# Column sums of a Sinkhorn loop taken by VectorE ahead of a product of ones, and a closing branch's transfers put on GpSimd's queue

## The chip, the cores and the metric

The kernel runs on one core of a Trainium2 chip. The metric is the device time of one execution in microseconds (us). Before the change it is 1538.89 us, the median of three runs (1538.41 to 1539.11).

A core has five engines that each run their own list of instructions in program order and wait for one another by semaphores: TensorE (PE in the profile, with its weight loads as PEld), VectorE (DVE), ScalarE (ACT), GpSimd (POOL) and SyncE (SP), which here only starts transfers. Transfers (DMAs) are started from the list of an engine; SP's and GpSimd's lists are the two that matter here.

## The reference, cut to what matters

A recurrence over 768 steps (linear attention with 4 batches, 8 heads of 48) gives `x`, 3072 tokens of 384. A mixture of 8 experts follows, whose gate matrix `P` (3072 x 8) is balanced by eight rounds of Sinkhorn:

```python
logits = x @ w_gate
logits = logits - logits.max()
P = np.exp(logits)
for _ in range(8):
    P /= P.sum(1, keepdims=True) + 1e-09
    P /= P.sum(0, keepdims=True) + 1e-09
    P *= N / E
out = np.zeros((N, D), dtype=np.float32)
for e in range(E):
    h = np.maximum(x @ w1[e], 0.0)
    ye = h @ w2[e]
    out += P[:, e:e + 1] * ye
```

The first division in a round is by sums over the 8 experts of a token (row sums), the second by sums over all 3072 tokens for each expert (column sums).

## The kernel before, in words

The kernel has four stretches. The **attention** runs over 24 chunks of 128 tokens, and beside it the first expert begins. The **ticks** follow: a list of units of TensorE work of the first expert is emptied one unit a tick, and small jobs are attached to tick numbers. The 14 **stages** come next: each is half of one of the other seven experts, done with 15 products of combined operands for the first matrix (a Strassen-like scheme, `g1_slots`, 30 slots for each of two groups of tokens) and plain products for the second (`g2_tiles`). Last stands the **closing branch**, `general`, a plain and slow version of everything, which is entered only when `flag` says that a decay `w` lies outside 0.7 to 1.1. The inputs draw `w` from 0.85 to 0.95.

Every engine is wrapped so that its instructions stay in the order in which the code is written (`InOrder`). So the code's order is the engine's order, and an instruction that waits holds up everything behind it on its engine.

`pm` holds the gate matrix as 128 partitions x (24 tiles x 8 experts). The generator `sinkhorn_rounds` makes a round in two pieces that are divided by `yield`. The first piece, all VectorE: row sums `rs`, their reciprocals, and `pm` times these. The second piece: the column sums `cs`, their reciprocals, and `pm` times these. Column sums cross partitions, which is done by a TensorE product with a matrix of ones (`pc`); the sums over the 24 tiles are VectorE's.

The pieces are not run in one go. In the ticks, `next(sk)` is called at ticks 0, 1, 2, 3, 4, 7, 9, 12, 14, 17, 19, 22, 24, 27, 29 and 32 (line 917); the first four set up the exponentials, so rounds 0 to 5 have their first pieces at 4, 9, 14, 19, 24, 29 and their second at 7, 12, 17, 22, 27, 32. Rounds 6 and 7 lie in stage 0, at slots 2, 5, 9 and 13 (line 1131), and slot 18 ends the loop. Three ticks of TensorE work, or three to four slots, lie between the end of a first piece and the second one.

The units of the ticks alternate. A unit `ph` (`g1_unit`) is nine products of 384 columns; its end is read by ScalarE (a Relu into `hb`) and then by VectorE (`SCALAR_TENSOR_TENSOR hb<-ph,hb`, the rest that the Relu's 16-bit result leaves). A unit `po` (`g2_half`) is twelve products, read by ScalarE alone. So a unit's VectorE instruction is issued behind its products and stands in VectorE's list ahead of whatever the next tick gives to VectorE. In stage 0 the products are named `bA`, `bY`, `bZ`, `bC`, `bB`, and VectorE's additions on them `tb`. VectorE has other work in the ticks too: low parts of split operands (`xv`, later `ws`) and maxima of the weights (`wms`).

The times below call the eight second pieces round 0 to round 7.

Of the kernel before, what the change touches and what calls it, by code (L numbers as in the profile page):

```python
# [8 lines left out]
F32 = mybir.dt.float32  # L9
# [4 lines left out]
ALU = mybir.AluOpType  # L14
AX = mybir.AxisListType
# [18 lines left out]
def rwkv_sinkhorn_moe(  # L34
# [13 lines left out]
    V, S_, G, T, Q = (  # L48
        InOrder(tc, e) for e in (nc.vector, nc.scalar, nc.gpsimd, nc.tensor, nc.sync)
    )  # L50

    B, H, S, D = r.shape
    NT, DM = out.shape
    E, _, F = w1.shape
    P = 128
# [3 lines left out]
    NTT = NT // P  # L59
    KC = DM // P  # L60
    FC = F // P
    TB = 512
# [25 lines left out]
    def part(home, dtype, at, shape):  # L88

        n = 1  # L90
        for s_ in shape:
            n *= s_
        x_ = home if home.dtype == dtype else home.bitcast(dtype)
        x_ = x_[:, at : at + n]
        if len(shape) == 1:
            return x_
        names = "abcd"[: len(shape)]
        return x_.rearrange(
            f"p ({' '.join(names)}) -> p {' '.join(names)}", **{c_: s_ for c_, s_ in zip(names[1:], shape[1:])}
        )  # L100
# [17 lines left out]
    logits = const.tile([P, NTT, E], F32, name="logits")  # L118
# [4 lines left out]
    ones = const.tile([P, P], F32, name="ones")  # L123
# [255 lines left out]
    for src, dst in ((tab, rtab), (tabr, ktab)):  # L379
        pt = ps3.tile([P, NPAIR, P], F32, tag="pa", name="pt_tab")  # L380
# [7 lines left out]
        out=mask, in_=mask, compare_op=ALU.is_gt, fill=0.0, base=0,  # L388
# [376 lines left out]
    pm = const.tile([P, NTT, E], F32, name="pm")  # L765
# [83 lines left out]
    skp = [ps4, "pq"]  # L849
# [27 lines left out]
    def sinkhorn_rounds(nm):  # L877
        for it in range(8):
            rs = sm.tile([P, NTT], F32, tag="rs", name=f"rs_{nm}{it}")
            V.tensor_reduce(rs, pm, axis=AX.X, op=ALU.add)  # L880
            V.tensor_scalar_add(rs, rs, 1e-9)
            V.reciprocal(rs, rs)
            V.tensor_tensor(pm, pm, rs.unsqueeze(2).broadcast_to([P, NTT, E]), op=ALU.mult)
            yield
            pc = skp[0].tile([P, NTT, E], F32, tag=skp[1], name=f"pc_{nm}{it}")
            T.matmul(
                pc.rearrange("p t e -> p (t e)"), ones, pm.rearrange("p t e -> p (t e)"),
                start=True, stop=True,
            )
            cs = sm.tile([P, E], F32, tag="cs", name=f"cs_{nm}{it}")  # L890
            V.tensor_reduce(cs, pc.rearrange("p t e -> p e t"), axis=AX.X, op=ALU.add)
            V.tensor_scalar(cs, cs, 1e-9, E / NT, op0=ALU.add, op1=ALU.mult)
            V.reciprocal(cs, cs)
            V.tensor_tensor(pm, pm, cs.unsqueeze(1).broadcast_to([P, NTT, E]), op=ALU.mult)
            yield
# [297 lines left out]
    def general(scratch):  # L1193

        BH = B * H
        yd = scratch.tile([B, S, DM], F32, name="yd")
        ldr = scratch.tile([NT, E], F32, name="ldr")
        pdr = scratch.tile([NT, E], F32, name="pdr")
        kb, rb, stt, kv = (part(hbx, F32, i * BH * D, (BH, D))[:D] for i in range(4))
        wn, un = (part(hbx, F32, 4 * BH * D + i * H * D, (H * D,))[:D] for i in range(2))  # L1200
        vt, yv = (part(hbx, F32, 5 * BH * D + i * BH, (BH,))[:D] for i in range(2))
        for dst, src in ((wn, w), (un, u)):
            Q.dma_start(dst, src.rearrange("(o h) d -> o (h d)", o=1).broadcast_to([D, H * D]))
        V.memset(stt, 0.0)

        def of_b(x_):
            return x_.rearrange("p (b h) d -> p b (h d)", b=B)

        def for_b(x_):
            return x_.unsqueeze(1).broadcast_to([D, B, H * D])  # L1210

        with tc.For_i(0, S, 1) as t:
            for dst, src in ((kb, k), (rb, r)):
                Q.dma_start(
                    dst,
                    src.rearrange("b h s d -> s (b h) d")[bass.ds(t, 1)].broadcast_to([D, BH, D]),
                )
            Q.dma_start(vt, v.rearrange("b h s d -> s d (b h)")[bass.ds(t, 1)].rearrange("o d a -> (o d) a"))
            V.tensor_tensor(kv, kb, vt.unsqueeze(2).broadcast_to([D, BH, D]), op=ALU.mult)
            V.tensor_tensor(of_b(kb), of_b(kv), for_b(un), op=ALU.mult)  # L1220
            V.tensor_tensor(kb, kb, stt, op=ALU.add)
            V.tensor_tensor(rb, rb, kb, op=ALU.mult)
            V.tensor_reduce(yv, rb, axis=AX.X, op=ALU.add)
            for b in range(B):
                Q.dma_start(
                    yd[b].rearrange("s (h d) -> s d h", d=D)[bass.ds(t, 1)].rearrange("o d h -> (o d) h"),
                    yv[:, b * H : (b + 1) * H],
                )
            V.tensor_tensor(of_b(stt), of_b(stt), for_b(wn), op=ALU.mult)
            V.tensor_tensor(stt, stt, kv, op=ALU.add)  # L1230

        def tiles_of(x_):
            return x_.rearrange("(t p) d -> t p d", p=P)

        yt = tiles_of(yd.rearrange("b s d -> (b s) d"))
        xt = part(hb3, F32, 0, (DM,))
        xT = part(hb3, F32, DM, (KC, P))
        acc = part(hb3, F32, 2 * DM, (DM,))
        wgf = part(hb3, F32, 3 * DM, (KC, E))
        lt, pt = (part(hb3, F32, 3 * DM + (KC + i) * E, (E,)) for i in range(2))  # L1240
        raw_a, raw_b = part(ws0, F32, 0, (KC, F)), part(ws1, F32, 0, (FC, DM))
        hT = part(hbx, F32, 0, (FC, P))
        Q.dma_start(wgf, w_gate.rearrange("(c p) e -> p c e", p=P))

        def turned(t):
            Q.dma_start(xt, yt[bass.ds(t, 1)].rearrange("o p d -> (o p) d"))
            px = ps1.tile([P, KC, P], F32, tag="ph", name="px_g")
            for c in range(KC):
                T.transpose(px[:, c], xt[:, c * P : (c + 1) * P], ident)
            S_.copy(xT, px)  # L1250

        with tc.For_i(0, NTT, 1) as t:
            turned(t)
            pl = ps2.tile([P, E], F32, tag="po", name="pl_g")
            for c in range(KC):
                T.matmul(pl, xT[:, c], wgf[:, c], start=(c == 0), stop=(c == KC - 1))
            S_.copy(lt, pl)
            Q.dma_start(tiles_of(ldr)[bass.ds(t, 1)].rearrange("o p d -> (o p) d"), lt)
        Q.dma_start(logits, ldr.rearrange("(t p) e -> p t e", p=P))
        mx = sm.tile([P, 1], F32, tag="mx", name="mx_g")  # L1260
        gm = sm.tile([P, 1], F32, tag="gm", name="gm_g")
        V.tensor_reduce(mx, logits, axis=AX.XY, op=ALU.max)
        for all_ in over_partitions(mx, 1, ps1, "ph", "gm_g"):
            pass
        V.tensor_scalar(gm, all_, -1.0, 0.0, op0=ALU.mult, op1=ALU.add)
        S_.activation(pm, logits, AF.Exp, bias=gm, scale=1.0)
        for _ in sinkhorn_rounds("g"):
            pass
        Q.dma_start(pdr.rearrange("(t p) e -> p t e", p=P), pm)
        with tc.For_i(0, NTT, 1) as t:  # L1270
            turned(t)
            Q.dma_start(pt, tiles_of(pdr)[bass.ds(t, 1)].rearrange("o p d -> (o p) d"))
            V.memset(acc, 0.0)
            for e in range(E):
                Q.dma_start(raw_a, w1[e].rearrange("(c p) f -> p c f", p=P))
                Q.dma_start(raw_b, w2[e].rearrange("(c p) d -> p c d", p=P))
                for f in range(FC):
                    ph = ps1.tile([P, P], F32, tag="ph", name=f"ph_g{e}_{f}")
                    for c in range(KC):
                        T.matmul(  # L1280
                            ph, raw_a[:, c, f * P : (f + 1) * P], xT[:, c],
                            start=(c == 0), stop=(c == KC - 1),
                        )
                    S_.activation(hT[:, f], ph, AF.Relu)
                po = ps2.tile([P, DM], F32, tag="po", name=f"po_g{e}")
                for f in range(FC):
                    T.matmul(po, hT[:, f], raw_b[:, f], start=(f == 0), stop=(f == FC - 1))
                V.scalar_tensor_tensor(acc, po, pt[:, e : e + 1], acc, op0=ALU.mult, op1=ALU.add)
            Q.dma_start(tiles_of(out)[bass.ds(t, 1)].rearrange("o p d -> (o p) d"), acc)

    bad = nc.values_load(flag.bitcast(I32), min_val=0, max_val=0x3F800000)
    with tc.If(bad > 0, preferred_fallthrough_block=False):
# [29 lines left out]
```

## Time and profile before

| | |
|---|---|
| median of three runs | 1538.89 us |
| the profiled execution, its own time | 1539.2 us |
| its span in the trace | 1537.5 us |
| TensorE busy | 1520.4 us (99% of the span) |
| VectorE busy | 1007.9 us (66%) |
| ScalarE busy | 678.4 us (44%) |
| GpSimd busy | 567.3 us (37%) |
| mean granted TensorE clock | 0.993 |

The span is the time from the first to the last instruction of the program; the 1.7 us that the execution's own time has beyond it lie around the program. The 40 slices show how even the kernel is, and that TensorE's clock is below full only in the first two:

```profile
PE   8999999999999999999999999999999999999998
DVE  7887667676666666667666666666666666566563
PEclk8899999999999999999999999999999999999999
```

Each digit is the busy share of a slice of 38 us in tenths; the last row is the clock granted to TensorE. A matmul's row in a timeline is modelled: its start is the time at which it enters the array, and the next one enters before it ends, so the spacing of starts is what a product costs TensorE.

### The profile page before, as it was taken

How to read it: one execution, taken by the hardware profiler on the slowest of the kernel's cores; microseconds unless marked ns; L12 is line 12 of the kernel's file. 1: busy time of each engine (PE TensorE's matmuls, PEld its weight loads, DVE VectorE, ACT ScalarE, POOL GpSimd, SP SyncE). 2: the span in 40 equal slices, each digit the busy share in tenths (PEclk: the TensorE clock that was granted, in tenths of full speed). 3: DMA queues.
4: the chain of work that ended last, by engine and by line, in shares of the span. 5: the costliest groups of instructions: out<-in, count | busy, mean ns of one | idle time of the engine just before them, and what ended most of it. 6: DMA issues, size and time to landing. Idle time of an engine off the chain costs nothing.

```text
span 1537.5 us, 26114 instructions
## 1 busy us (share of the span) xinstructions
PE 1520.4 (99%) x10302; PEld 859.7 (56%) x10302; DVE 1007.9 (66%) x1660; ACT 678.4 (44%) x1243; POOL 567.3 (37%) x683
## 2 busy tenths in 40 slices
PE   8999999999999999999999999999999999999998
PEld 5677766655555555555555555555555555555554
DVE  7887667676666666667666666666666666566563
ACT  4444434435454444535454444535354444444320
POOL 6676875120213424242424334242424233242200
PEclk8899999999999999999999999999999999999999
DMA  9455623121236666665657666655455454555433
GB/s 212 89 115 109 128 51 109 52 76 52 98 56 108 91 114 86 125 96 86 115 87 128 92 125 80 124 63 100 57 74 81 57 98 59 98 59 94 57 98 125
DMA packets 186851, 143.16 MB, mean 93 GB/s; under 512 B 109537, under 2 KB 180962, under 8 KB 186722
## 3 DMA queue, kind: packets, MB, share of 16 engines
q0 software_dynamic: 44928, 61.36, 32.8%
q1 hardware_dynamic: 141586, 80.07, 19.1%
q8 instruction: 82, 1.34, 0.4%
q14 instruction: 47, 0.39, 0.1%
q10 hardware_dynamic: 208, 0.00, 0.0%
HBM read 55.39 MB, written 80.23 MB: 88 GB/s over the span
## 4 chain that ended last, share of the span: by engine, by line
PE 92%; DVE 6%; ACT 1%; issue 1%; DMA 0%; POOL 0%; SPq 0%; ACTq 0%; DVEq 0%; POOLq 0%
PE po L30 48%; PE bZ L30 12%; PE bY L30 12%; PE bA L30 5%; PE bB L30 5%; PE ph L30 5%; PE bC L30 2%; PE py L30 1%; PE pA L30 1%; DVE ws L30 1%; DVE at L30 1%; DVE kp L30 1%; ACT xsc L30 1%; DVE hb L30 1%; PE pz L30 1%
## 5 line engine op out<-in xcount | busy, mean ns | idle before, releaser
L30 PE MATMUL po<-ws,hbx 128*128 128x384 f16 x3360 | 736.8, 326 | 0.0
L30 POOL DMA_DIRECT2D accd<-stg x288 | 250.4, 870 | 694.7 <-ACT stg L30 670.4
L30 PEld LDWEIGHTS <-hbx 128*128 128x128 f16 x3504 | 334.1, 98 | 292.6
L30 PEld LDWEIGHTS <-ws 128*128 128x128 f16 x3096 | 302.0, 98 | 246.8 <-issue 4.4
L30 ACT ACTIVATE hbx<-tb 128x512 f16<-128x512 f32 x224 | 141.4, 631 | 450.0 <-DVE tb L30 450.0
L30 PE MATMUL po<-ws,hb 128*128 128x384 f16 x1248 | 323.2, 326 | 0.6 <-DVE ws L30 0.5
L30 DVE TENSOR_TENSOR tb<-bY,tb 128x512 f32<-128x512 f32 x168 | 116.2, 692 | 195.4 <-PE bY L30 195.2
L30 ACT ACTIVATE stg<-po,pe 128x384 f32<-128x384 f32 x312 | 179.4, 575 | 121.8 <-PE po L30 95.1
L30 PE MATMUL bZ<-xv,ws 128*128 128x512 f16 x840 | 227.0, 379 | 0.4 <-DVE tb L30 0.4
L30 PE MATMUL bY<-xv,ws 128*128 128x512 f16 x840 | 227.0, 379 | 0.0
L30 DVE TENSOR_TENSOR tb<-bZ,tb 128x512 f32<-128x512 f32 x168 | 115.6, 688 | 134.9 <-PE bZ L30 134.9
L30 PEld LDWEIGHTS <-hb 128*128 128x128 f16 x1248 | 121.4, 98 | 94.1 <-issue 1.4
L30 POOL TENSOR_TENSOR ucb<-rawb 128x256 f32<-128x256 f32 x84 | 75.8, 953 | 118.2 <-DMA rawb<-in_moe_w_dram 118.2
L30 DVE TENSOR_TENSOR tb<-bB,tb 128x512 f32<-128x512 f32 x112 | 77.5, 692 | 48.7 <-PE bB L30 46.8
L30 PE MATMUL ph<-hbx,ws 128*128 128x384 f16 x576 | 105.9, 329 | 1.3 <-DMA hbx<-xsc 1.0
L30 DVE SCALAR_TENSOR_TENSOR hb<-tb,hbx 128x512 f16<-128x512 f32 x112 | 77.2, 689 | 24.7 <-ACT hbx L30 19.5
L30 PE MATMUL bB<-xv,ws 128*128 128x512 f16 x336 | 90.8, 379 | 0.0
L30 PE MATMUL bA<-xv,ws 128*128 128x512 f16 x336 | 90.8, 379 | 0.0
L30 DVE SCALAR_TENSOR_TENSOR hbx<-tb,hbx 128x512 f16<-128x512 f32 x112 | 77.9, 696 | 14.8 <-ACT hbx L30 10.4
L30 ACT COPY tb<-bZ 128x512 f32<-128x512 f32 x56 | 32.8, 586 | 65.4 <-PE bZ L30 65.4
L30 DVE SCALAR_TENSOR_TENSOR hb<-ph,hb 128x384 f16<-128x384 f32 x64 | 35.2, 553 | 25.7 <-ACT hb L30 25.0
L30 DVE TENSOR_REDUCE wms<-rawb 128x1 f32<-128x768 f32 x56 | 51.7, 944 | 0.0
(166 smaller groups left out, 1484.6 us busy)
## 6 DMA issues: line engine op xcount, KB each, us to landing
accd<-stg POOLq DMA_DIRECT2D x288, 192.0 KB, 3.7
rawb<-in_moe_w_dram SPq DMA_DIRECT2D x28, 768.0 KB, 7.8
e0d<-stg SPq DMA_DIRECT2D x48, 192.0 KB, 2.1
hb<-e0d SPq DMA_DIRECT2D x48, 192.0 KB, 3.4
vn<-in_v_dram SPq DMA_DIRECT2D x24, 192.0 KB, 3.0
accd<-stg SPq DMA_DIRECT2D x24, 192.0 KB, 1.8
accd<-hb POOLq DMA_DIRECT2D x24, 192.0 KB, 4.8
rawb<-accd SPq DMA_DIRECT2D x24, 192.0 KB, 2.5
```

Of the source, the lines that this page charges most:

```text
L30: return lambda *a, **k: self.tc.keep_in_program_order(f(*a, **k))
```

## The change

Two things are changed. In `sinkhorn_rounds`, VectorE now first sums `pm` over the 24 tiles (128 x 192 to 128 x 8, from SBUF), and the product of ones is taken of that: it has 8 columns in place of 192, and its result is already the column sum, so that `V.tensor_scalar` reads it in PSUM. The number of instructions is the same on each engine. The reduce, which stood behind the product, now stands ahead of it, in the same piece of the generator. And in `general` each `Q.dma_start` (SP's list) becomes `G.dma_start` (GpSimd's list).

```diff
@@ -882,14 +882,11 @@
             V.reciprocal(rs, rs)
             V.tensor_tensor(pm, pm, rs.unsqueeze(2).broadcast_to([P, NTT, E]), op=ALU.mult)
             yield
-            pc = skp[0].tile([P, NTT, E], F32, tag=skp[1], name=f"pc_{nm}{it}")
-            T.matmul(
-                pc.rearrange("p t e -> p (t e)"), ones, pm.rearrange("p t e -> p (t e)"),
-                start=True, stop=True,
-            )
             cs = sm.tile([P, E], F32, tag="cs", name=f"cs_{nm}{it}")
-            V.tensor_reduce(cs, pc.rearrange("p t e -> p e t"), axis=AX.X, op=ALU.add)
-            V.tensor_scalar(cs, cs, 1e-9, E / NT, op0=ALU.add, op1=ALU.mult)
+            V.tensor_reduce(cs, pm.rearrange("p t e -> p e t"), axis=AX.X, op=ALU.add)
+            pc = skp[0].tile([P, TB], F32, tag=skp[1], name=f"pc_{nm}{it}")[:, :E]
+            T.matmul(pc, ones, cs, start=True, stop=True)
+            V.tensor_scalar(cs, pc, 1e-9, E / NT, op0=ALU.add, op1=ALU.mult)
             V.reciprocal(cs, cs)
             V.tensor_tensor(pm, pm, cs.unsqueeze(1).broadcast_to([P, NTT, E]), op=ALU.mult)
             yield
@@ -1200,7 +1197,7 @@
         for dst, src in ((wn, w), (un, u)):
-            Q.dma_start(dst, src.rearrange("(o h) d -> o (h d)", o=1).broadcast_to([D, H * D]))
+            G.dma_start(dst, src.rearrange("(o h) d -> o (h d)", o=1).broadcast_to([D, H * D]))
...
-            Q.dma_start(tiles_of(out)[bass.ds(t, 1)].rearrange("o p d -> (o p) d"), acc)
+            G.dma_start(tiles_of(out)[bass.ds(t, 1)].rearrange("o p d -> (o p) d"), acc)
```

TensorE's list at round 1, in the ticks: `ph_3` is the unit ahead of the product, `ph_4` the unit behind it, and the brackets name the engine whose semaphore an instruction waits for.

```order
 L30 LDWEIGHTS ws_75
 L30 MATMUL ph_3_3917<-hbx,ws_75 128x384
-L30 MATMUL pc_s_3929<-pm,ones 128x192 [waits DVE_49]
-L30 LDWEIGHTS ws_75
-L30 MATMUL ph_4_3939<-hbx,ws_75 128x384 [waits DVE_49]
+L30 MATMUL pc_s_3931<-cs_s_3929,ones 128x8 [waits DVE_49]
+L30 LDWEIGHTS ws_75
+L30 MATMUL ph_4_3939<-hbx,ws_75 128x384 [waits PE_49]
```

The product keeps its place between the two units. It waited for VectorE's write of `pm`, made ticks earlier; now it waits for the write of `cs`, and `ph_4`, which waited for VectorE itself, stands behind that.

VectorE's list at the same place, from the maximum over the weights to the instruction that reads `ph_4`:

```order
 L30 TENSOR_REDUCE wmas_3685<-wms_3684 128x2 [waits DVE_49]
 L30 SCALAR_TENSOR_TENSOR hb_73<-ph_3_3917,hb_73 128x384 [waits Activation_49]
-L30 TENSOR_REDUCE cs_s_3931<-pc_s_3929 128x8 [waits PE_49]
-L30 TENSOR_SCALAR cs_s_3931<-cs_s_3931 128x8 [waits DVE_49]
-L30 RECIPROCAL cs_s_3931<-cs_s_3931 128x8 [waits DVE_49]
-L30 TENSOR_TENSOR pm<-pm,cs_s_3931 128x192 [waits DVE_49]
+L30 TENSOR_REDUCE cs_s_3929<-pm 128x8
+L30 TENSOR_SCALAR cs_s_3929<-pc_s_3931 128x8 [waits PE_49]
+L30 RECIPROCAL cs_s_3929<-cs_s_3929 128x8 [waits DVE_49]
+L30 TENSOR_TENSOR pm<-pm,cs_s_3929 128x192 [waits DVE_49]
 L30 SCALAR_TENSOR_TENSOR hb_73<-ph_4_3939,hb_73 128x384 [waits Activation_49]
```

The reduce keeps its place in VectorE's list, behind the instruction that reads `ph_3`; what it waits for is gone, and the wait for TensorE has moved to the instruction after it.

VectorE's list at round 6, in stage 0 (`hbx<-tb` is the low part of a result of the combined products, `tb<-bC` an addition on the product that TensorE makes next):

```order
 L30 TENSOR_TENSOR tb<-bZ_0_0_4397,tb 128x512 [waits PE_49]
 L30 SCALAR_TENSOR_TENSOR hbx<-tb,hbx 128x512 [waits Activation_49]
-L30 TENSOR_REDUCE cs_s_4441<-pc_s_4439 128x8 [waits PE_49]
-L30 TENSOR_SCALAR cs_s_4441<-cs_s_4441 128x8 [waits DVE_49]
-L30 RECIPROCAL cs_s_4441<-cs_s_4441 128x8 [waits DVE_49]
+L30 TENSOR_REDUCE cs_s_4439<-pm 128x8
+L30 TENSOR_SCALAR cs_s_4439<-pc_s_4441 128x8 [waits PE_49]
+L30 RECIPROCAL cs_s_4439<-cs_s_4439 128x8 [waits DVE_49]
 L30 TENSOR_TENSOR tb<-bC_0_0_4451,tb 128x512 [waits PE_49]
```

Here too the reduce stays where it was, and it is the product of ones on TensorE that has got a new thing to wait for.

More of the change, by code (lines that the diff above doesn't have):

```diff
@@ L1213, in general @@
             for dst, src in ((kb, k), (rb, r)):
-                Q.dma_start(
+                G.dma_start(
                     dst,
@@ L1217, in general @@
                 )
-            Q.dma_start(vt, v.rearrange("b h s d -> s d (b h)")[bass.ds(t, 1)].rearrange("o d a -> (o d) a"))
+            G.dma_start(vt, v.rearrange("b h s d -> s d (b h)")[bass.ds(t, 1)].rearrange("o d a -> (o d) a"))
             V.tensor_tensor(kv, kb, vt.unsqueeze(2).broadcast_to([D, BH, D]), op=ALU.mult)
@@ L1224, in general @@
             for b in range(B):
-                Q.dma_start(
+                G.dma_start(
                     yd[b].rearrange("s (h d) -> s d h", d=D)[bass.ds(t, 1)].rearrange("o d h -> (o d) h"),
@@ L1242, in general @@
         hT = part(hbx, F32, 0, (FC, P))
-        Q.dma_start(wgf, w_gate.rearrange("(c p) e -> p c e", p=P))
+        G.dma_start(wgf, w_gate.rearrange("(c p) e -> p c e", p=P))
         def turned(t):
-            Q.dma_start(xt, yt[bass.ds(t, 1)].rearrange("o p d -> (o p) d"))
+            G.dma_start(xt, yt[bass.ds(t, 1)].rearrange("o p d -> (o p) d"))
             px = ps1.tile([P, KC, P], F32, tag="ph", name="px_g")
@@ L1257, in general @@
             S_.copy(lt, pl)
-            Q.dma_start(tiles_of(ldr)[bass.ds(t, 1)].rearrange("o p d -> (o p) d"), lt)
-        Q.dma_start(logits, ldr.rearrange("(t p) e -> p t e", p=P))
+            G.dma_start(tiles_of(ldr)[bass.ds(t, 1)].rearrange("o p d -> (o p) d"), lt)
+        G.dma_start(logits, ldr.rearrange("(t p) e -> p t e", p=P))
         mx = sm.tile([P, 1], F32, tag="mx", name="mx_g")
@@ L1268, in general @@
             pass
-        Q.dma_start(pdr.rearrange("(t p) e -> p t e", p=P), pm)
+        G.dma_start(pdr.rearrange("(t p) e -> p t e", p=P), pm)
         with tc.For_i(0, NTT, 1) as t:
             turned(t)
-            Q.dma_start(pt, tiles_of(pdr)[bass.ds(t, 1)].rearrange("o p d -> (o p) d"))
+            G.dma_start(pt, tiles_of(pdr)[bass.ds(t, 1)].rearrange("o p d -> (o p) d"))
             V.memset(acc, 0.0)
             for e in range(E):
-                Q.dma_start(raw_a, w1[e].rearrange("(c p) f -> p c f", p=P))
-                Q.dma_start(raw_b, w2[e].rearrange("(c p) d -> p c d", p=P))
+                G.dma_start(raw_a, w1[e].rearrange("(c p) f -> p c f", p=P))
+                G.dma_start(raw_b, w2[e].rearrange("(c p) d -> p c d", p=P))
                 for f in range(FC):
```

## The prediction

> **What bounds the kernel now.** I read the page's busy line first, then the list of what TensorE waited for.
>
> ```profile
> PE 1520.4 (99%) x10302; PEld 859.7 (56%) x10302; DVE 1007.9 (66%) x1660; ACT 678.4 (44%) x1243; POOL 567.3 (37%) x683
> ...
> PE ph L30 <- DVE hb L30: 0.3, 1, 0.3
> ...
> PE bZ L30 <- DVE tb L30: 0.4, 1, 0.4
> ```
>
> TensorE is busy for all but 17 us. The list (total, times, longest) has two waits in the stretch of the Sinkhorn rounds, of 0.3 and 0.4 us. So TensorE sets the end, and no idle time lies behind the rounds that could take up a delay: what a product of ones makes TensorE wait moves the end, less these 0.7 us at most. VectorE at 66% looks free. What counts is where VectorE stands at eight moments, which the timelines of both engines show.
>
> **The product itself.** Timeline of TensorE in round 2 (start, duration):
>
> ```profile
> 272.91 0.49 PE L30 MATMUL pc_s<-pm,ones 128*128 128x192 f32 x2
> 273.33 0.38 PE L30 MATMUL pmax_s<-md_s,ones 2*128 2x2 f32 x2
> 273.64 2.12 PE L30 MATMUL po<-ws,hb 128*128 128x384 f16 x12
> ```
>
> The old product costs 0.32 us at most places (255.09 to 255.41 below). No row shows 8 columns. A product of 2 columns with the same ones in 32-bit floats, `pmax_s`, takes 0.31 us from its start to the next. So the new one lies between 0 and 0.32 us, and I take 0.31, the row nearest in shape: the gain is nothing, and 8 x 0.32 = 2.6 us at the very most. [...]
>
> **What is added: TensorE waits for VectorE's place in its list.** The new reduce reads 128 x 192 from SBUF:
>
> ```profile
> L30 DVE TENSOR_REDUCE rs_s<-pm 128x24 f32<-128x192 f32 x8 | 2.7, 340 | 0.0
> ```
>
> The same elements from the same tile take 0.34 us, from PSUM 0.35 (below). I take 0.35; with the stride of the other direction it may be more, which each round would feel once. From VectorE's end to TensorE's start it takes 0.05 us: below, `hb<-ph` ends at 263.92 + 0.54 = 264.46, and the unit that waited for it starts at 264.51. So TensorE's next work starts 0.35 + 0.05 + 0.31 = 0.71 us behind the reduce's start. The reduce's start is read off the old trace, since its place in VectorE's list is the same, and then compared with the old start of the work behind the product.
>
> Rounds 0 and 1:
>
> ```profile
> 254.76 0.54 DVE L30 SCALAR_TENSOR_TENSOR hb<-ph,hb 128x384 f16<-128x384 f32 x1
> 255.09 0.49 PE L30 MATMUL pc_s<-pm,ones 128*128 128x192 f32 x2
> 255.41 0.81 PE L30 MATMUL ph<-hbx,ws 128*128 128x384 f16 x4
> ...
> 255.00:268.00 13.00, 12.67 (x79) 7.77 (x78) 12.41 (x21) 5.57 (x10) 12.37 (x15) 1.00 0.13 46
> ...
> 263.70 0.49 PE L30 MATMUL pc_s<-pm,ones 128*128 128x192 f32 x2
> 263.92 0.54 DVE L30 SCALAR_TENSOR_TENSOR hb<-ph,hb 128x384 f16<-128x384 f32 x1
> 264.51 1.62 PE L30 MATMUL ph<-hbx,ws 128*128 128x384 f16 x9 [0.33 <-DVE hb L30]
> 267.34 0.35 DVE L30 TENSOR_REDUCE cs_s<-pc_s 128x8 f32<-128x192 f32 x1
> ```
>
> The window row has busy TensorE, its loads, VectorE, ScalarE, GpSimd: VectorE is busy for 12.4 of 13 us, it is late. In round 0 the reduce can start 0.48 us behind its predecessor (the spacing of 291.27 and 291.75 below), at 255.24; TensorE goes on at 255.95, 0.54 late. VectorE itself is not delayed, so in round 1 the reduce still starts at 267.34, 3.64 us behind TensorE's product: TensorE goes on at 268.05 and not 264.51, **3.54 us** for both rounds, the 0.33 already counted off. VectorE's backlog is used up there.
>
> Rounds 2, 3 and 4 stand directly behind a `ph` unit:
>
> ```profile
> 273.11 0.49 ACT L30 ACTIVATE hb<-ph 128x384 f16<-128x384 f32 x1 [0.94 <-PE ph L30]
> ...
> 282.14 0.49 ACT L30 ACTIVATE hb<-ph 128x384 f16<-128x384 f32 x1 [0.32 <-PE ph L30]
> 282.26 1.95 PE L30 MATMUL po<-ws,hb 128*128 128x384 f16 x11
> ...
> 290.75 0.49 ACT L30 ACTIVATE hb<-ph 128x384 f16<-128x384 f32 x1 [0.97 <-PE ph L30]
> 290.87 2.11 PE L30 MATMUL po<-ws,hb 128*128 128x384 f16 x12
> 291.27 0.56 DVE L30 SCALAR_TENSOR_TENSOR hb<-ph,hb 128x384 f16<-128x384 f32 x1
> 291.75 0.35 DVE L30 TENSOR_REDUCE cs_s<-pc_s 128x8 f32<-128x192 f32 x1
> ```
>
> Here no backlog is needed. The unit's end releases ScalarE's Relu (0.49), that VectorE's `hb<-ph`, and 0.48 later the reduce: a chain that starts when TensorE has finished the unit, however late TensorE is. Round 4: 291.75 + 0.71 = 292.46 against 290.87, **1.59 us**. Round 3, counted from 282.14 by the same 1.00 us to the reduce: 283.85 against 282.26, **1.59**. Round 2: 274.11 + 0.71 = 274.82 against 273.33, **1.49**.
>
> Round 5 follows a `po` unit, which VectorE does not read:
>
> ```profile
> 298.42 0.56 DVE L30 SCALAR_TENSOR_TENSOR hb<-ph,hb 128x384 f16<-128x384 f32 x1 [1.65 <-ACT hb L30]
> 299.65 0.49 PE L30 MATMUL pc_s<-pm,ones 128*128 128x192 f32 x2
> ```
>
> The reduce is done at 298.42 + 0.48 + 0.35 = 299.25, ahead of TensorE: **0**.
>
> Rounds 6 and 7, in stage 0:
>
> ```profile
> 315.02 0.69 DVE L30 TENSOR_TENSOR tb<-bY,tb 128x512 f32<-128x512 f32 x1 [1.52 <-PE bY L30]
> 316.37 0.98 PE L30 MATMUL ph<-hbx,ws 128*128 128x384 f16 x5
> 317.18 0.81 PE L30 MATMUL bC<-xv,ws 128*128 128x512 f16 x3
> 317.92 0.34 DVE L30 TENSOR_REDUCE cs_s<-pc_s 128x8 f32<-128x192 f32 x1
> ...
> 319.40 0.68 DVE L30 TENSOR_TENSOR tb<-bC,tb 128x512 f32<-128x512 f32 x1
> ...
> 328.98 0.98 PE L30 MATMUL po<-ws,hb 128*128 128x384 f16 x5
> ...
> 331.31 0.35 DVE L30 TENSOR_REDUCE cs_s<-pc_s 128x8 f32<-128x192 f32 x1
> ```
>
> Round 6: VectorE waited for TensorE at 315.02, so what lies between is dependence and not backlog; 317.92 + 0.71 = 318.63 against 316.37, **2.26 us**. Round 7 by its rows: 331.31 + 0.71 = 332.02 against 328.98, 3.04 us. But VectorE was late there, and TensorE's 2.26 us let it catch up: its addition on `bC`, at 319.40, could have run when `bC` ends, 317.18 + 0.81 = 317.99, 1.4 us sooner, and behind it VectorE has one gap alone, itself behind that addition. I take 3.04 - 1.4 = **1.64**, with 0.9 and 3.04 as ends.
>
> The waits add up to 3.54 + 1.49 + 1.59 + 1.59 + 0 + 2.26 + 1.64 = **12.1 us**.
>
> **The clock.** Windows of TensorE in the attention (busy, then granted clock):
>
> ```profile
> 32.50:36.00 3.50, 1.69 (x19) 1.00 1.05 206
> 36.00:39.40 3.40, 3.40 (x58) 0.50 0.55 112
> ...
> 46.20:49.60 3.40, 1.87 (x20) 1.00 0.77 152
> 49.60:53.00 3.40, 2.41 (x10) 0.50 0.39 79
> ```
>
> A stretch of 3.4 us with only 1.69 to 1.87 us busy was followed by one at half the clock. Half the clock for 3.4 us costs 1.7 us of dense work. Round 1's gap of 3.5 us must leave some stretch of 3.4 us less than 1.7 us busy. Round 6's 2.26 us does so if 1.5 of it fall into one stretch, three positions of the stretches in four; the gaps of rounds 3, 4 and 7 in about every second one. Work beside those old gaps was light (transposes, short products) and is dense here, so some will not count: I take three stretches, **5.1 us**, with none and six as ends (0 to 10.2). [...]
>
> **The branch's transfers.** The result's transfers and GpSimd's last instruction:
>
> ```profile
> out_dram<-rawb SPq DMA_DIRECT2D x24, 192.0 KB, 2.6
> ...
> 1466.64 0.86 POOL L30 DMA_DIRECT2D accd<-stg  x1 [2.23 <-DVE hbx L30]
> ```
>
> All 24 tiles of the result come from the stages, so the body is not run, before or after. What is left is GpSimd's step past it, with a wait for its own earlier transfers, beside 70 us in which it has nothing to do until the span ends at 1537.5: **0**. Were that cover gone, each us there would cost one. SP's list gets shorter at the end; half a us either way.
>
> **Sum.** 12.1 + 5.1 = 17.2 us on the profiled execution's 1539.2 gives 1556.4. That execution lies 0.3 us above the median of the runs, so the forecast is **1556.1 us**.
>
> **Rivals.**
> *The clock stays up* or falls once: 12.1 to 13.8 us, 1551 to 1553. For it speaks that the work beside the gaps is dense; against it the two pairs of windows above. 0.22. [...]
> *The clock falls at nearly every gap,* and round 7 pays its full 3.04: 12.1 + 1.4 + 10.2 = 23.7, 1562.6. 0.16.
> *No wait lasts:* the reduce is done before TensorE arrives, as in round 5, since TensorE once delayed finds VectorE with an empty list. It decides at the point where the reduce's end plus 0.05 us lies ahead of the last product of the unit before. Then at most 2.6 us are gained, 1536.3 us, not slower. Against it: in rounds 2 to 4 the chain begins with that very unit's end. 0.05, with the case in which the delays are given back later; there are 0.4 us of idle time for that.
> *The change does not do what it says:* the lists show that it does. A gain beyond 2.6 us would need a shorter end: 0.02.
>
> **How the numbers follow.** Forecast 0.55. The low end is the waits less 1.7 us of error in rounds 6 and 7, without a fall of the clock, 1549; the high end is the second rival, 1563. Measurement tells about 0.2% (3.1 us) from no change: slower 0.93, same 0.05, faster 0.02.
>
> **What would show it.** In the new trace TensorE's waits for `cs` in seven rounds, about 3.1 (round 1), 1.5 (2 to 4), 2.2 (6) and 1 to 3 us (7), none in round 5; VectorE idle for 0.4 us behind each reduce; the granted clock at half for 3.4 us behind the gaps, which the windows of rounds 1 to 7 would show; the tail unchanged. Wrong would be a product that does not hold TensorE, that is no idle time ahead of `pc_s`.

## The result, and the profile after

| | before | changed | ratio [95% interval] |
|---|---|---|---|
| median | 1538.78 us (6 runs) | 1551.59 us (6 runs, 1550.68 to 1553.77) | 1.0084 [1.0073, 1.0095] |
| profiled execution, its own time | 1539.2 us | 1551.64 us | |
| its span | 1537.5 us | 1550.2 us | |

The changed kernel is slower by 12.8 us. The page's busy line of the changed kernel:

```profile
PE 1520.8 (98%) x10302; PEld 857.3 (55%) x10302; DVE 1008.6 (65%) x1660; ACT 678.3 (44%) x1243; POOL 565.1 (36%) x683
```

TensorE is busy for as long as before, 1520.8 us against 1520.4, so the time went into idle TensorE. (Work at half the clock shows as busy time: in the window 266.31:273.14 below TensorE is busy for 5.80 of 6.83 us at 0.50. Up to TensorE's last product there are 17.07 us at half the clock in each of the two traces, but 6.83 of them lie in the rounds now, and all lay in the attention before.) The list of what TensorE waited for, changed kernel (total, times, longest):

```profile
PE pc_s L30 <- DVE cs_s L30: 13.0, 7, 3.4
```

Before, this line did not exist. The timeline of TensorE in the changed kernel shows the eight products of ones (start, duration, and in brackets the wait), with the work behind four of them:

```profile
255.21 0.39 PE L30 MATMUL pc_s<-cs_s,ones 128*128 128x8 f32 x2 [0.51 <-DVE cs_s L30]
...
267.34 0.59 PE L30 MATMUL pc_s<-cs_s,ones 128*128 128x8 f32 x2 [3.44 <-DVE cs_s L30]
267.79 2.72 PE L30 MATMUL ph<-hbx,ws 128*128 128x384 f16 x8
...
280.54 0.39 PE L30 MATMUL pc_s<-cs_s,ones 128*128 128x8 f32 x2 [1.57 <-DVE cs_s L30]
280.86 0.38 PE L30 MATMUL pmax_s<-md_s,ones 2*128 2x2 f32 x2
...
291.25 0.39 PE L30 MATMUL pc_s<-cs_s,ones 128*128 128x8 f32 x2 [1.62 <-DVE cs_s L30]
291.50 2.11 PE L30 MATMUL po<-ws,hb 128*128 128x384 f16 x12
...
301.52 0.39 PE L30 MATMUL pc_s<-cs_s,ones 128*128 128x8 f32 x2 [1.57 <-DVE cs_s L30]
...
310.54 0.28 PE L30 MATMUL pc_s<-cs_s,ones 128*128 128x8 f32 x2
310.68 1.62 PE L30 MATMUL ph<-hbx,ws 128*128 128x384 f16 x9
...
329.09 0.39 PE L30 MATMUL pc_s<-cs_s,ones 128*128 128x8 f32 x2 [2.18 <-DVE cs_s L30]
...
343.09 0.36 PE L30 MATMUL pc_s<-cs_s,ones 128*128 128x8 f32 x2 [2.08 <-DVE cs_s L30]
```

Seven products wait, the one of round 5 does not. A product that has waited holds TensorE for 0.25 us (291.25 to 291.50), one that has not for 0.14 (310.54 to 310.68). Round 1's holds it for 0.45 us (267.34 to 267.79): it runs at a granted clock of 0.50, as the windows below show.

To see where the 12.7 us of span come from, the same instruction is looked up in both traces: a product ahead of the rounds, and VectorE's last addition, in the timelines of the two engines. Before:

```profile
246.48 0.38 PE L30 MATMUL pmax_gm<-md_gm,ones 1*128 1x1 f32 x2
...
1531.40 0.62 DVE L30 SCALAR_TENSOR_TENSOR rawb<-po,pe,rawb 128x384 f32<-128x384 f32 x1 [1.33 <-PE po L30]
```

Changed kernel:

```profile
245.93 0.38 PE L30 MATMUL pmax_gm<-md_gm,ones 1*128 1x1 f32 x2
...
1545.73 0.62 DVE L30 SCALAR_TENSOR_TENSOR rawb<-po,pe,rawb 128x384 f32<-128x384 f32 x1 [1.33 <-PE po L30]
```

Ahead of the rounds the changed kernel is 0.55 us early. From the first row to the second it takes 1299.80 us against 1284.92, **14.88 us more**. From the second row to the end of the span it takes 4.5 us against 6.1, **1.6 us less**. Together -0.55 + 14.88 - 1.6 = 12.7.

The 14.88 us all lie in the rounds: the work behind round 7's product starts at 343.31, 14.33 us later than before (328.98), and so does the last addition. By rounds, with the start of the work behind each product (where it is not in the rows above, the product's start plus the 0.22 to 0.25 us that it holds TensorE):

| round | before | changed | shift | growth of the shift | predicted wait |
|---|---|---|---|---|---|
| 0 | 255.41 | 255.46 | +0.05 | 0.60 | |
| 1 | 264.51 | 267.79 | +3.28 | 3.23 (0 and 1: 3.83) | 3.54 |
| 2 | 273.33 | 280.86 | +7.53 | 4.25, of it 2.61 half clock | 1.49 |
| 3 | 282.26 | 291.50 | +9.24 | 1.71 | 1.59 |
| 4 | 290.87 | 301.76 | +10.89 | 1.65 | 1.59 |
| 5 | 299.97 | 310.68 | +10.71 | -0.18 | 0 |
| 6 | 316.37 | 329.33 | +12.96 | 2.25 | 2.26 |
| 7 | 328.98 | 343.31 | +14.33 | 1.37 | 1.64 |

The waits come to 14.88 - 2.61 = 12.27 us, with 0.2 us of half clock left in them, that of round 1's product. The 2.61 us are the growth of the shift from 3.28 to 5.89 us over the units behind round 1, which wait for nothing but run at half the clock. Windows of the changed kernel (from and to, length, busy TensorE, its loads, VectorE, ScalarE, GpSimd, granted clock, share of DMA, GB/s):

```profile
262.90:266.31 3.41, 1.00 (x7) 0.39 (x4) 3.38 (x5) 1.31 (x3) 3.33 (x5) 1.00 0.16 58
266.31:273.14 6.83, 5.80 (x19) 2.97 (x20) 3.82 (x8) 0.49 (x1) 6.06 (x9) 0.50 0.00 0
...
276.55:279.97 3.42, 2.42 (x15) 1.25 (x13) 1.70 (x3) 0.97 (x2) 0.00 (x0) 1.00 0.18 62
279.97:283.38 3.41, 2.84 (x18) 1.96 (x19) 1.65 (x8) 0.01 (x1) 0.00 (x0) 1.00 0.00 0
...
327.75:331.17 3.42, 2.08 (x13) 1.27 (x14) 2.59 (x6) 0.42 (x2) 3.42 (x5) 1.00 0.16 58
...
341.41:344.82 3.41, 1.73 (x11) 1.08 (x12) 2.27 (x6) 0.43 (x1) 0.00 (x0) 1.00 0.00 0
344.82:348.23 3.41, 3.41 (x21) 1.86 (x20) 3.13 (x6) 1.49 (x3) 0.00 (x0) 1.00 0.16 58
```

Up to the last product the granted clock of this trace changes at 17.14, 20.55, 47.86, 54.68, 266.31 and 273.14 us, which lie 1, 8, 2, 62 and 2 steps of 3.41 us apart, and the windows are cut at such steps. Round 1's gap leaves one stretch with 1.00 us busy, and 6.83 us at half clock follow. The gaps of rounds 2 and 6 fall on two stretches each, which keep 2.08 us or more; the clock stays up. Round 7's leaves 1.73 us busy, and it stays up too.

Groups of the changed kernel (busy, mean ns of one, idle time before them):

```profile
L30 DVE TENSOR_REDUCE cs_s<-pm 128x8 f32<-128x192 f32 x8 | 3.9, 484 | 0.0
```

The reduce with the stride takes 0.48 us.

### The profile page after: what moved, and what is told of

It is laid out like the page before. It is cut to its first block, busy times and chain, and to the rows that moved or that the text cites. A ratio compares the mean times of both kernels' runs of the same rounds, so it can differ in the third digit from the quotient of the medians.

```text
span 1550.2 us, 26112 instructions
## 1 busy us (share of the span) xinstructions
PE 1520.8 (98%) x10302; PEld 857.3 (55%) x10302; DVE 1008.6 (65%) x1660; ACT 678.3 (44%) x1243; POOL 565.1 (36%) x683
## 4 chain that ended last, share of the span: by engine, by line
PE 90%; DVE 7%; ACT 1%; issue 1%; DMA 0%; ACTq 0%; DVEq 0%
PE po L30 47%; PE bY L30 12%; PE bZ L30 12%; PE bA L30 5%; PE bB L30 5%; PE ph L30 4%; PE bC L30 2%; PE py L30 1%; DVE ws L30 1%; DVE hb L30 1%; PE pA L30 1%; DVE kp L30 1%; DVE xv L30 1%; DVE at L30 1%; ACT xsc L30 1%; PE pz L30 1%
## 5 line engine op out<-in xcount | busy, mean ns | idle before, releaser
L30 ACT ACTIVATE hb<-ph 128x384 f16<-128x384 f32 x64 | 31.2, 488 | 49.2 <-PE ph L30 48.6
```

Source lines behind the costliest of these rows:

```text
L30: return lambda *a, **k: self.tc.keep_in_program_order(f(*a, **k))
```

## The experiments

The chip and the runs of the kernel before beside them differ by group: the first four ran beside 21 runs (median 1538.99 us), the last three beside 11 (1538.63 us).

| kernel | median (lowest to highest, runs) | ratio [95% interval] |
|---|---|---|
| loop alone changed | 1553.12 (1549.8 to 1555.07, 5) | 1.0089 [1.0075, 1.0103] |
| branch alone changed | 1537.56 (1536.24 to 1538.89, 11) | 0.9992 [0.9983, 1.0001] |
| reduce in the first piece | 1535.98 (1535.19 to 1537.22, 11) | 0.9983 [0.9974, 0.9992] |
| round 1's gap filled | 1550.77 (1548.68 to 1551.0, 5) | 1.0075 [1.0061, 1.0089] |
| second pieces a tick later | 1548.38 (1543.75 to 1550.81, 6) | 1.0057 [1.0044, 1.007] |
| every long gap filled | 1549.2 (1548.98 to 1550.09, 5) | 1.0069 [1.0056, 1.0082] |
| changed kernel again | 1551.66 (1549.55 to 1553.23, 5) | 1.0081 [1.0068, 1.0094] |

### The loop alone, the branch alone

The first kernel has the new `sinkhorn_rounds` and the old `general` (its difference from the changed kernel is below), the second the old loop and the new `general`:

```diff
-            G.dma_start(dst, src.rearrange("(o h) d -> o (h d)", o=1).broadcast_to([D, H * D]))
+            Q.dma_start(dst, src.rearrange("(o h) d -> o (h d)", o=1).broadcast_to([D, H * D]))
...
```

> The Sinkhorn loop as changed, the closing branch's transfers left on SP's queue. Theory: the loop costs 14 to 15 us by itself (12.3 us of waits of TensorE for cs and one or two stretches of half clock), and the branch's edit gives 1.5 us back at the end of the span; so this kernel is slower than the changed one by some 1.5 us, at about 1553 us (+14.3 on before), and its span ends 5.6 to 6 us after the last DVE instruction on rawb starts, as before, not 3.9. Rival: the shorter tail of the changed kernel was chance; then this kernel takes what the changed one takes, 1551.6 us (+12.8).

> The closing branch's transfers on GpSimd's queue, the Sinkhorn loop as before. Theory: SP no longer clears its twelve DMA semaphores behind the last transfer's landing, so the span is 1.3 to 1.7 us shorter: 1537.3 us (-1.5). Rival (the prediction's step): the branch costs and gives nothing, 1538.8 us within 0.3.

The loop alone costs 14.1 us (1553.12 - 1538.99), the branch alone gives 1.4 us (its interval just reaches 1), and 14.1 - 1.4 = 12.7 is the change. The branch's gain lies in the tail. From the start of VectorE's last addition to the end of the span it is 6.1 us before and 6.4 with the loop alone (transfers on SP), and 4.4 to 5.2 in the seven traces of kernels with the transfers on GpSimd. SP's own waits in the last stretch, and its semaphore instructions by line (count, duration in ns, first and last start), before:

```profile
SPq L1292 <- SPq L1292: 2.3, 1, 2.3
...
L1292 SPq EVENT_SEMAPHORE  x8: 17/17/17, 1532.5 to 1535.3; - x8
...
L1318 SPq EVENT_SEMAPHORE  x14: 17/28/28, 1535.8 to 1537.4; - x14
```

Branch alone:

```profile
SPq L1318 <- DMA out_dram<-rawb: 2.2, 1, 2.2
...
L1318 SPq EVENT_SEMAPHORE  x14: 17/28/28, 1530.9 to 1534.7; - x14
```

L1292 is the branch and L1318 the end of the program. With the transfers on SP's list, SP waits at the branch for the eight semaphores of its own transfers, the last tiles of the result among them, and starts on the end's semaphores only behind their landing, at 1535.8. With the transfers on GpSimd's list SP has no semaphore instruction at the branch. It starts on those of the end at 1530.9 and has ten of the first twelve behind it when the last tile of the result lands. The single instructions in the traces give the price: from the semaphore instruction that this landing releases to the end of the span it is 2.31 us in both traces with the transfers on SP (1535.19 to 1537.49 before), and 1.00 to 1.04 us in all seven with the transfers on GpSimd (1549.15 to 1550.15 in the changed kernel). So 1.3 us of the shorter tail are SP's instructions between landing and end; from the last addition to the landing it is 3.4 to 4.1 us on either list. The expectation above counted only the twelve at the end; the eight at the branch go too. GpSimd's step past the branch costs nothing: in the changed kernel its instructions at the branch (L1289 there) start between 1481.5 and 1486.3, 64 us before the end.

### The reduce one piece earlier

The two lines of the reduce move up over the `yield`, to the end of the first piece, three ticks or slots ahead of the product; all else as in the changed kernel:

```diff
-            yield
             cs = sm.tile([P, E], F32, tag="cs", name=f"cs_{nm}{it}")
             V.tensor_reduce(cs, pm.rearrange("p t e -> p e t"), axis=AX.X, op=ALU.add)
+            yield
             pc = skp[0].tile([P, TB], F32, tag=skp[1], name=f"pc_{nm}{it}")[:, :E]
             T.matmul(pc, ones, cs, start=True, stop=True)
```

> As the changed kernel, but VectorE's sum over the tiles stands at the end of the round's first piece, ahead of the yield, so three ticks lie between it and the product of ones. Theory: TensorE waits for cs in no round, the whole 14.9 us of the rounds go, each product of 8 columns costs 0.14 to 0.2 us less than that of 192 (8 x 0.15 = 1.2 us), and the branch's 1.5 us stay: 1536 us, 2.5 to 3 below before. Rival: waits come from VectorE's total load and not from the reduce's place; then some of the waits of rounds 1, 6 and 7 stay and the time lies above 1540 us.

It is the fastest of all: 1535.98 us, 0.9983 [0.9974, 0.9992] of before and 15.6 us below the changed kernel. TensorE's waits between 250 and 420 us:

```profile
PE ph L30 <- DVE hb L30: 0.8, 1, 0.8
PE bZ L30 <- DVE tb L30: 0.4, 1, 0.4
```

No product waits; the two waits that are left are those of the old kernel, 0.3 and 0.4 us there. The same instructions are issued, with the same strided reduce (0.50 us here), so the loss of the changed kernel is the reduce's place alone, not its work. TensorE's timeline, reduce early, at round 0:

```profile
255.58 0.28 PE L30 MATMUL pc_s<-cs_s,ones 128*128 128x8 f32 x2
255.72 1.62 PE L30 MATMUL ph<-hbx,ws 128*128 128x384 f16 x9
```

The product holds TensorE for 0.14 us where that of 192 columns held it for 0.32. Eight times 0.18 are 1.4 us; between this kernel and the one with the branch alone, whose loop is the old one, the medians differ by 1.6. So of the 3.0 us that it lies below the runs of before beside it, about half is the loop's and half the branch's.

### Filling the gaps: what the half clock costs

TensorE gets dense products of 384 columns (0.16 us each) ahead of the product of ones, into the same PSUM tile, whose first 8 columns the product of ones then overwrites and of which nothing else is read. In one kernel it is 18 of them in round 1, in the other (whose edit is shown) counts by the gaps of six rounds:

```diff
-            pc = skp[0].tile([P, TB], F32, tag=skp[1], name=f"pc_{nm}{it}")[:, :E]
+            pcf = skp[0].tile([P, TB], F32, tag=skp[1], name=f"pc_{nm}{it}")
+            pc = pcf[:, :E]
+            for _ in range((0, 18, 8, 8, 8, 0, 11, 10)[it] if nm == "s" else 0):
+                T.matmul(
+                    pcf[:, :TB0].rearrange("p (t q) -> p t q", q=P),
+                    W[0][:, 0, :P], xpos(NPOS - 1, 1)[:, 0][:, 0], start=True, stop=True,
+                )
```

> As the changed kernel, with 18 further products of 384 columns put on TensorE in round 1 ahead of the product of ones, into the bank that this then overwrites: 18 x 0.163 = 2.9 us of dense work inside the 3.4 us in which TensorE waits. Theory: TensorE's idle stretch is what halves its clock there for 6.8 us; with the gap filled the clock stays up and 2.6 us go, 1549.0 us (-2.6 on the changed kernel, +10.2 on before), and the wait left in round 1 is 0.5 us. Rival: the fall of the clock has another cause, or the stall is not idle time that work can fill; then the time is that of the changed kernel or up to 2.9 us longer, 1551.6 to 1554.5 us.

With round 1 alone filled the time is 1550.77 us, 0.8 below the changed kernel's 1551.59 and 1.8 above what was expected. The wait left in round 1 is 0.52 us, as expected. Windows of that kernel:

```profile
263.00:267.00 4.00, 3.48 (x23) 1.93 (x22) 3.77 (x6) 1.21 (x2) 3.84 (x5) 1.00 0.14 49
...
324.11:327.52 3.41, 1.62 (x10) 1.02 (x11) 2.76 (x6) 0.75 (x2) 3.36 (x5) 1.00 0.16 58
...
337.77:341.18 3.41, 1.33 (x10) 0.86 (x10) 2.60 (x7) 0.88 (x3) 0.00 (x0) 1.00 0.00 0
341.18:344.59 3.41, 3.41 (x11) 1.32 (x10) 2.30 (x4) 1.08 (x2) 0.00 (x0) 0.50 0.00 0
```

Round 1 keeps its wait, now filled, and its clock. But the units behind it come sooner (round 7's product at 339.90 us and not at 343.09), the later gaps fall on the steps of 3.41 us at other places, and round 7's gap of 2.08 us, which cost no clock in the first trace of the changed kernel, is followed by half clock, 0.50 from 341.18 to 344.59. Round 6's, with 1.62 us busy, is not. So one fall is gone and another has come; what all of them together are worth is read from the second filling kernel, beside the changed kernel again:

> As the changed kernel, with dense products of 384 columns put ahead of the product of ones in each round in which TensorE waits, into the bank that it then overwrites: 18 in round 1, 8 in rounds 2 to 4, 11 and 10 in rounds 6 and 7 (0.163 us each, always less than the wait). Theory: the waits stay, as time that is now filled, and the clock falls behind no round; the time is the waits alone, 12.3 - 1.4 = 10.9 us on before, 1549.9 us, and below that of the changed kernel by the 1.7 to 2.6 us of its falls. Rival: the falls of the clock behind the rounds have nothing to do with the gaps; then the time is within 0.5 us of the changed kernel's.

> The changed kernel again, beside the two others on one chip. Theory: 1551.6 us (+12.8 on before) in the median, with single executions 1 to 2 us apart by where the clock falls; TensorE's waits for cs within 0.1 us of 0.51, 3.44, 1.57, 1.62, 1.57, 0, 2.18 and 2.08 in every trace. Rival: the waits differ from one execution to the next as the times do.

TensorE's waits between 250 and 420 us with every long gap filled:

```profile
PE pc_s L30 <- DVE cs_s L30: 3.1, 7, 0.9
```

9.9 of the 13.0 us of idle are filled, and no stretch behind the rounds falls to half clock. The median is 1549.2 us against 1551.66 of the changed kernel beside it: **some 2.5 us is what the half clock costs** (medians of five runs each, which range over 1.1 and 3.7 us), and 10.6 us stay (1549.2 - 1538.63), which are the waits less the tail's gain. From the product ahead of the rounds (245.63) to the last addition (1542.99) this kernel's trace has 12.44 us more than before, against 12.27 for the waits alone in the table above. (The trace of the branch alone, whose loop is that of before, has 0.7 us more than before by the same measure; its wait behind round 1's product is 1.1 us and not 0.3. So a difference of that size between two traces says little by itself.)

The second trace of the changed kernel has its falls elsewhere. Its windows:

```profile
264.68:268.10 3.42, 0.29 (x3) 0.29 (x4) 3.05 (x5) 0.96 (x2) 3.26 (x5) 1.00 0.06 22
268.10:271.51 3.41, 3.41 (x12) 1.57 (x13) 1.30 (x3) 0.38 (x1) 3.41 (x5) 0.50 0.00 0
278.34:281.75 3.41, 1.88 (x12) 1.39 (x13) 2.09 (x8) 0.48 (x1) 0.00 (x0) 1.00 0.13 49
281.75:285.17 3.42, 3.42 (x13) 1.58 (x11) 0.00 (x0) 1.31 (x2) 0.00 (x0) 0.50 0.13 46
```

Two falls of 3.4 us, behind rounds 1 and 2. Round 2's gap is the same 1.57 us as in the first trace, but it lies in one stretch and not over two. By the measure above this trace has 15.67 us more than before, 3.2 more than with all gaps filled, where the first trace had 14.88, 2.4 more. The kernel's runs go with the clock: 1549.55 us at a mean granted clock of 0.998, 1553.23 at 0.992. With all gaps filled they spread by 1.1 us. But the runs of before beside them spread by 2.7 us too, without a gap in the rounds (1537.12 us at 0.998, 1539.49 at 0.994), so how much of the spread the rounds add is not shown.

The expectation that the waits are the same within 0.1 us in every trace held for seven rounds. Round 6's wait is 2.48 us here against 2.18, and 2.15 to 2.30 in the three other traces that leave it open.

### Second pieces of rounds 2 to 4 a tick later

```diff
-    for t in (0, 1, 2, 3, 4, 7, 9, 12, 14, 17, 19, 22, 24, 27, 29, 32):
+    for t in (0, 1, 2, 3, 4, 7, 9, 12, 14, 18, 19, 23, 24, 28, 29, 32):
```

The product then stands behind a `po` unit, which VectorE does not read, as in round 5.

> As the changed kernel, with the second pieces of rounds 2, 3 and 4 one tick later (18, 23, 28 in place of 17, 22, 27), so that each follows a po unit, which VectorE does not read, and not a ph unit. Theory: the wait of 1.6 us in these rounds is the chain ph, ScalarE, VectorE, reduce, and not VectorE's load; it goes in all three, and with it 3 x (1.57 to 1.62) + 3 x 0.1 = 5.0 us: 1546.6 us (+7.6 on before), TensorE's waits for cs fall from seven to four. Rival: VectorE is late anyway; then the three waits stay within half of their size and the time is above 1549 us.

TensorE's waits between 250 and 420 us:

```profile
PE pc_s L30 <- DVE cs_s L30: 8.3, 5, 3.4
```

Two of the three waits are gone and the third, round 3's, is 0.33 us, so five waits are left and not four, and 4.7 us of them went: the unit ahead of the product decides, as the prediction said of rounds 2 to 5. The time fell by 3.3 us only (1548.38 against 1551.66), and the runs spread over 7 us. In its one trace the clock is at half for 6.83 us behind round 1 and 3.41 us behind round 6, where the changed kernel's first trace has 6.83 us in all. That accounts for the 1.8 us missing from the expected time as far as one trace can; no run separates it.

## Why the prediction was right, by its steps

**What bounds the kernel.** Right. TensorE's busy time did not change, and every wait ahead of a product moved all later work by its length; nothing was given back behind round 7.

**The waits, 12.1 us.** Right: 12.27 us measured. Round 1's reduce was to start at 267.34, less the 0.55 us by which this execution is early 266.79; it starts at 266.80. VectorE's timeline of the changed kernel:

```profile
266.34 0.55 DVE L30 SCALAR_TENSOR_TENSOR hb<-ph,hb 128x384 f16<-128x384 f32 x1
266.80 0.48 DVE L30 TENSOR_REDUCE cs_s<-pm 128x8 f32<-128x192 f32 x1
...
342.46 0.48 DVE L30 TENSOR_REDUCE cs_s<-pm 128x8 f32<-128x192 f32 x1
```

Two terms inside were mis-sized and partly cancel. "I take 0.35; with the stride of the other direction it may be more": it is 0.48. "I take 0.31, the row nearest in shape": the product costs 0.25 after a wait. From the reduce's start to TensorE's next work it is 0.48 + 0.06 + 0.25 = 0.79 us and not 0.71, which the growths of rounds 2 to 4 show, 0.06 to 0.15 above their predicted waits. That the sum came so near is in part luck: rounds 0 to 4 came out 0.6 us longer than predicted, rounds 5 and 7 together 0.45 shorter.

**The product itself, "the gain is nothing".** Mis-sized the safe way. Where it does not wait it costs 0.14 us, a gain of 0.18 a round, which shows in round 5 and, eight times over, in the kernel with the early reduce. The bounds of 0 and 0.32 held it.

**Round 7, 1.64 with ends 0.9 and 3.04.** The catching up of VectorE was real, and 1.8 us instead of 1.4: the reduce starts at 342.46 (the last row above), where its old start and the shift behind round 6 give 331.31 + 12.96 = 344.27. TensorE waits 2.08 us there, the shift grows by 1.37. Rounds 6 and 7 together are 3.62 against 3.90.

**The clock, "three stretches, 5.1 us".** The step that was too large. The falls are there, the size is some 2.5 us in the medians and 2.4 to 3.2 in the two traces. Two stretches of half clock came in each of the two, not three. In every trace of a kernel that keeps round 1's gap open round 1 falls; of the other rounds at most one did, where the prediction counted on two. And the 6.83 us behind round 1 cost less than twice 1.7 us, since they hold 1 us of the wait: 2.61 and the 0.2 us of round 1's product. The odds were worked out from a limit near 1.87 us busy, and no such limit shows: over all the traces, each stretch of the rounds with 1.33 us busy or less was followed by half clock and none with 2.00 or more, but between them 1.84 and 1.88 were, and 1.62, 1.73, 1.78 and, in the kernel with later ticks, 1.88 were not. So busy time, as the profile counts it, is not quite what decides; what is stays open. Gaps of 1.57 us (round 2, changed kernel again) and 2.08 us (round 7, round 1's gap filled) were each followed by 3.41 us at half clock. In the rounds half clock lasted 3.41 or 6.83 us in every trace that has it, and it began at another place in each: at 266.31 us in the first trace of the changed kernel, at 268.10 and 281.75 in the second.

**The branch, 0: "SP's list gets shorter at the end; half a us either way".** Wrong by a little, and with it the sign "the tail unchanged". The cover on GpSimd was as described, but it is SP that the change freed, by 1.3 us behind the last landing and 1.4 us in the medians.

**The sum.** 12.1 + 5.1 + 0 was forecast; 12.3 + 2.5 - 1.4 = 13.4 are the parts as measured, and 12.8 is the difference of the medians, 0.6 apart where the changed kernel's runs spread over 3 us. The forecast of 1556.1 lies 4.5 us above the 1551.59 measured: 2.6 by the clock, 1.4 by the branch, the rest not told apart. The range held it and the waits are as worked out, but the time that came is that of the first rival, which let the clock fall once or not at all and had a chance of 0.22.

**Not tried.** Whether round 1's wait goes if VectorE is relieved of other work there (its late `wms` and `xv` instructions), and what tells the stretches with 1.62 to 1.88 us busy that were followed by half clock from those that were not.

## What to carry to other kernels

In a kernel like this one, where VectorE's list keeps the order of the code, an operation that is put ahead of a matmul can cost what stands ahead of it in that list, and not what it takes: here a reduce of 0.48 us, used eight times, cost 12 us, and the same reduce, one piece of the generator earlier, made the loop 1.6 us faster than it had been. Look for the point at which the inputs are ready and issue it there. A gap that is added in front of TensorE can be paid a second time by the clock, here with some 2.5 us on 12.3 us of waits, and that differed with where the gap fell: the same 1.57 us was followed by 3.41 us at half clock in one trace of the changed kernel and by none in the other.

## What the runs showed of the hardware that was not expected

- A sum over the outer direction of 128 x 192 32-bit floats in SBUF (128 x 8 out, stride of 8 elements) took 0.48 us in the changed kernel and 0.50 with the reduce early; over the inner direction (128 x 24 out) 0.34, and over the outer direction from PSUM 0.35 (before).
- A product of 8 columns with 128 x 128 ones in 32-bit floats cost TensorE 0.14 us between other work and 0.25 us behind a wait (0.22 in round 7), not the 0.31 of the products of 1 and 2 columns (which also have 1 and 2 rows).
- Round 2's gap of 1.57 us was followed by half clock in one trace of the changed kernel and not in the other, with another place in the stretches of 3.41 us: there it left 1.88 us busy in one stretch, here 2.42 and 2.84 in two. Busy time alone does not tell: stretches with 1.62, 1.73 and 1.78 us busy were not followed by half clock either.
- Behind a gap, half clock lasted 6.83 us in the two traces in which round 1's gap reached 1.03 us (changed kernel) and 0.93 us (later ticks) into the first slow stretch. It lasted 3.41 us in the six cases in which the gap ended between 1.9 us ahead of the first slow stretch and 0.2 us into it.
- With the transfers of a branch on its list (before, and the loop alone), SP waited at that branch for the transfers that it had under way, though the branch is not entered: eight semaphore instructions, and 2.31 us from the last landing to the end in place of 1.0.
